# A written job list for the first seven blocks of an attention-and-two-MLPs kernel, two-place stores of split weights, and joined first loads

## The chip, the cores and the metric

The kernel runs on one core of a Trainium2 chip. A core has five engines that run their own queues of instructions in order and wait for each other by semaphores: TensorE (PE, with its weight loads PEld), VectorE (DVE), ScalarE (ACT), GpSimd (POOL) and SyncE (SP), which here issues DMAs. ACT can issue DMAs too. The metric is the device time of one execution in microseconds.

## The reference

Linear attention is followed by two MLPs. All arrays are float32.

```python
# q, k, v: (8 batches, 8 heads, 576, 64)
q_s = exp(q - max(q, -1)); q_s /= sum(q_s, -1) + 1e-9
k_s = exp(k - max(k, 2));  k_s /= sum(k_s, 2) + 1e-9
kv = einsum('bhsd,bhse->bhde', k_s, v)
attn = einsum('bhsd,bhde->bhse', q_s, kv)
x = attn.transpose(0, 2, 1, 3).reshape(4608, 512)
h = x @ w_in                          # (512, 2048)
x = (h * clip(h + 3, 0, 6) / 6) @ w_out      # first MLP
h = x @ w2_in
out = (h * sigmoid(h)) @ w2_out              # second MLP
```

## The kernel before

**Tiling.** The 4608 tokens are nine blocks (j) of 512. A unit u = 4j + pair is two heads of one block: its q, its share of k and v, and the kv product. One MLP step (phase, j, f) takes one of 16 slices of 128 hidden features: `mm1` makes h of the slice with 12 matmuls (four column groups c, three products each, since a float32 operand is held as an upper and a lower part), a gate makes g from h, and `mm2` adds the slice to the block's result with 12 matmuls.

**Stages.** `first_block` runs the attention of the first units, turns the first MLP's 32 weight tiles from float32 into parts, and runs steps (0, 0, f). `middle` runs blocks 1 to 6 and meanwhile prepares the second MLP's weights: sums of quarters of the matrices, split in parts and stored in the DRAM buffer `ws`. From block 4 on, x goes through DRAM too (`x_store`, `load_x`), then is split by ACT (`x_high`) and DVE (`x_low`). `second_mlp` does the rest in a seven-product form and is not touched.

**What sets the order.** `first_block` and `middle` write their work as jobs of a `Plan`: engine, time, key, function, jobs that must be done first. `Plan.run` plays the jobs through with these times, tries 400 random changes of the keys, and calls the functions in the best order that it found. Each engine then works off its instructions in that order.

**A unit's steps.** DVE takes the maxima (`q_max` L419, `k_max` L349 to L351); PE turns k's maxima (L356) and spreads them (L368); DVE and ACT make the exponentials (L377, L387); POOL subtracts and scales q (L427, L453); PE turns q (L461) and ACT copies it (L486); PE makes kv (L397), ACT scales it (L414), and PE makes x (`x_mm`, L495). ACT copies x's upper part (`x_upper`, L509). Its lower part comes in one of two ways: DVE subtracts (`x_lower`, L514, for the units in `DIRECT_X`), or PE adds minus the upper part into the same PSUM bank (`x_rest`, L522) and ACT copies what is left (`x_lower_copy`, L529). A gate has the same two ways: `lower` (L572, DVE, for the f in `DIRECT_G`) or `rest` (L584, PE) and `lower_copy` (L589, ACT). Before that, ACT applies relu (L554), DVE multiplies (`times_h`, L578) and ACT copies the upper part (L569).

**A weight tile's conversion.** ACT scales its two halves (L120, L124), DVE shifts, rounds and sets the sign (L132, L139, L143), ACT copies the upper part (L160), and DVE or, for the numbers in `ASIDE`, POOL subtracts for the lower part (L164).

**Loads.** k and v come in 512 rows and a tail of 64 rows, so a unit is one DMA for k, one for its tail, one for q, two for v and one for its tail: 256 + 64 + 256 + 256 + 64 = 896 KB. Units 2 and 3 go into the tile `ahead`. The weight tiles follow, 512 KB each.

**Spare matmuls.** `spin` puts matmuls without use (tile `busy`, L849) into the start.

## Time and profile before

| | us |
|---|---|
| median of 3 runs | 1578.11 (1577.84 to 1581.05) |
| profiled execution | 1579.01 |
| its span, first to last instruction | 1577.0 |
| PE busy | 1558.9 |
| DVE busy | 1111.1 |
| ACT busy | 761.6 |
| POOL busy | 487.8 |

The span is what the trace covers; the profiled execution is 2.0 us longer. Busy shares are averages over stages that differ much, so they have to be read by stage. A matmul's row lasts longer than the distance to the next one, since they overlap: it is the distance that counts in a row of matmuls. The same holds for DVE and ACT, where the next instruction can start before the last one's row has ended.

### The profile page before, as it was taken

The numbers are of one execution on the slowest core, as the hardware profiler recorded it, in microseconds if no ns is written. First come the engines' busy times: TensorE is split into PE (matmuls) and PEld (weight loads), VectorE is DVE, ScalarE is ACT, GpSimd is POOL, SyncE is SP. The second block draws the span as 40 slices with busy tenths as digits, with TensorE's granted clock in tenths as the row PEclk, the third lists the DMA queues.
The fourth block names the chain that finished last, engine by engine and source line by source line (L and its number), as shares of the span: only waits on it lengthen the run. The fifth ranks groups of instructions, "written<-read, shape, count | busy, mean of one in ns | idle before, by whom it ended". The sixth has DMA issues, their size and how long they took to land.

```text
span 1577.0 us, 22414 instructions
## 1 busy us (share of the span) xinstructions
PE 1558.9 (99%) x7352; PEld 1268.4 (80%) x7352; DVE 1111.1 (70%) x1792; ACT 761.6 (48%) x1360; POOL 487.8 (31%) x442
## 2 busy tenths in 40 slices
PE   7999999999999999999999999999999999999998
PEld 4777878887878888888888888888888888888887
DVE  7988577776767776554689569846986697677632
ACT  6886245454555554443365236533643464345322
POOL 4334224433424335321232243323223422440000
PEclk9999999999999999999999999999999999999999
DMA  9915977777778875755666786766668875879850
GB/s 267 345 44 185 313 216 227 238 215 215 223 215 246 235 227 166 238 174 193 192 222 218 214 226 224 249 217 192 237 203 218 220 252 192 227 226 370 260 127 27
DMA packets 391203, 342.82 MB, mean 217 GB/s; under 512 B 184880, under 2 KB 297520, under 8 KB 391088
## 3 DMA queue, kind: packets, MB, share of 16 engines
q1 hardware_dynamic: 389040, 340.32, 70.3%
q8 instruction: 58, 0.95, 0.2%
q10 hardware_dynamic: 2048, 1.08, 0.2%
q14 instruction: 57, 0.47, 0.1%
HBM read 247.20 MB, written 94.11 MB: 216 GB/s over the span
## 4 chain that ended last, share of the span: by engine, by line
PE 92%; DMA 2%; issue 1%; DVE 1%; POOL 1%; ACT 1%; SPq 1%; ACTq 0%; POOLq 0%; DVEq 0%
PE pb L1340 24%; PE pb L1499 24%; PE h L541 20%; PE y L613 17%; PE y L615 3%; PE pa L495 2%; PE pa L397 2%; DMA qraw<-in_q_dram 1%; DMA xr<-xq 0%; DMA xq<-xq 0%; POOL wi L164 0%; SPq L232 0%; PE pa L368 0%; PE pa L356 0%; ACT r L554 0%
## 5 line engine op out<-in xcount | busy, mean ns | idle before, releaser
L541 PE MATMUL h<-x,wi 128*128 128x512 f32 x1536 | 382.5, 396 | 1.6 <-POOL wi L164 0.9
L1340 PE MATMUL pb<-xo,ring 128*128 128x512 f32 x1680 | 383.0, 389 | 0.0
L1499 PE MATMUL pb<-gsp,ring 128*128 128x512 f32 x1680 | 382.4, 389 | 0.0
L1340 PEld LDWEIGHTS pb<-xo,ring 128*128 128x128 f32 x1680 | 315.4, 188 | 65.8 <-issue 0.5
L1499 PEld LDWEIGHTS pb<-gsp,ring 128*128 128x128 f32 x1680 | 315.4, 188 | 65.4
L541 PEld LDWEIGHTS h<-x,wi 128*128 128x128 f32 x1536 | 283.5, 188 | 65.9 <-POOL wi L164 2.0
L613 PE MATMUL y<-g,wo 128*128 128x512 f32 x1344 | 323.9, 390 | 0.6 <-ACT g L569 0.6
L613 PEld LDWEIGHTS y<-g,wo 128*128 128x128 f32 x1344 | 251.4, 188 | 53.6 <-ACT g L569 1.1
L1327 DVE TENSOR_TENSOR gsp<-g,gsp 128x512 fp32r<-128x512 f32 x240 | 183.0, 782 | 26.0 <-ACT gsp L1445 25.2
L1445 ACT CAST gsp<-g 128x512 fp32r<-128x512 f32 x240 | 143.6, 621 | 106.2 <-PE pb L1499 88.3
L578 DVE SCALAR_TENSOR_TENSOR h<-r,h 128x512 f32<-128x512 f32 x112 | 77.4, 691 | 80.3 <-ACT r L554 80.1
L554 ACT ACTIVATE r<-h 128x512 f32<-128x512 f32 x112 | 67.0, 598 | 133.4 <-PE h L541 131.7
L1327 POOL TENSOR_TENSOR xst<-xst 128x512 f32<-128x512 f32 x32 | 72.1, 2254 | 167.4 <-DVE xo L1327 85.3
L1327 DVE TENSOR_TENSOR g<-r,pb 128x512 f32<-128x512 f32 x96 | 65.7, 684 | 54.6 <-ACT r L1354 54.1
L1354 ACT ACTIVATE r<-pb 128x512 f32<-128x512 f32 x96 | 57.1, 595 | 97.0 <-DVE pb L1327 72.8
L1327 POOL TENSOR_TENSOR g<-g 128x512 f32<-128x512 f32 x40 | 53.6, 1340 | 148.6 <-DVE g L1327 123.4
L1327 POOL TENSOR_TENSOR s<-U,s 128x512 f32<-128x512 f32 x32 | 42.6, 1331 | 173.1 <-DVE U L1327 173.1
L569 ACT CAST g<-h 128x512 fp32r<-128x512 f32 x112 | 65.6, 586 | 59.8 <-DVE h L578 51.5
L572 DVE TENSOR_TENSOR g<-h,g 128x512 fp32r<-128x512 f32 x97 | 66.7, 688 | 28.8 <-ACT g L569 27.3
L1327 DVE TENSOR_TENSOR U<-pb,s 128x512 f32<-128x512 f32 x80 | 55.0, 688 | 17.0 <-PE pb L1340 14.9
L194 POOL TENSOR_TENSOR fa<-fa 128x256 f32<-128x256 f32 x64 | 49.9, 780 | 43.7 <-DVE sp L226 28.5
L427 POOL TENSOR_TENSOR qe<-qraw,qm 128x512 f32<-128x512 f32 x34 | 37.9, 1114 | 79.4 <-DVE qz L469 46.0
(158 smaller groups left out, 1721.2 us busy)
## 6 DMA issues: line engine op xcount, KB each, us to landing
ring<-ws SPq DMA_DIRECT2D x280, 512.0 KB, 3.9
ws<-sp SPq DMA_DIRECT2D x256, 128.0 KB, 2.6
wi_early<-in_moe_w_in_dram SPq DMA_DIRECT2D x16, 512.0 KB, 8.6
wo_early<-in_moe_w_out_dram SPq DMA_DIRECT2D x16, 512.0 KB, 9.6
wi_raw<-in_moe_w_in_dram SPq DMA_DIRECT2D x16, 512.0 KB, 5.0
ws<-w_sum SPq DMA_DIRECT2D x64, 128.0 KB, 2.2
ws<-fa SPq DMA_DIRECT2D x64, 128.0 KB, 2.3
wo_raw<-in_moe_w_out_dram SPq DMA_DIRECT2D x16, 512.0 KB, 4.4
```

The lines of the kernel that those rows point to most:

```text
L194: lambda to=to, x=x, y=y, op=op: nc.gpsimd.tensor_tensor(out=at[to], in0=at[x], in1=at[y], op=op)
L541: nc.tensor.matmul(h, w[:, a, c, :], x[:, e, c, :], start=(c == 0 and n == 0), stop=(c == NC - 1 and n == 2),)
L554: nc.scalar.activation(self.r, self.h, AF.Relu, bias=3.0)
L569: nc.scalar.copy(self.g[:, 0], self.r)
L572: nc.vector.tensor_tensor(out=self.g[:, 1], in0=self.r, in1=f32(self.g[:, 0]), op=ALU.subtract)
L578: nc.vector.scalar_tensor_tensor(out=self.h, in0=self.r, scalar=6.0, in1=self.h, op0=ALU.min, op1=ALU.mult)
L613: nc.tensor.matmul(y[c], w[:, a, cs], g[:, e, :], start=st, stop=sp)
L1327: (eng or nc.vector).tensor_tensor(out=out, in0=a, in1=b, op=how)
L1340: nc.tensor.matmul(to, ws_[:, a], e[:, c], start=p in ("P1", "P6", "P5") and c == 0 and m == 0, stop=c == 1 and m == 2, skip_group_check=True,
L1354: nc.scalar.activation(r, d[b, n, key], AF.Sigmoid)
L1445: nc.scalar.copy(t[0], source(p, i))
L1499: nc.tensor.matmul(d[b, p][m], w[:, a, m * P : (m + 1) * P], t[e], start=new and i == 0 and k == 0, stop=i == NPR - 1 and k == 2, skip_gro ...
```

## The change

The order is no longer searched. `FIRST` and `MIDDLE` are written lists of job numbers, two signs for each job, and `run` calls the jobs in that order. The order has been found outside of the kernel. With it go four other edits. More of the lower parts are subtracted by DVE: `DIRECT_X` has six units instead of two, `DIRECT_G` eleven f instead of one, and `ASIDE` gives POOL 18 weight tiles instead of 16. `store` of a split weight writes the two places in `ws` of one part in one DMA of 256 KB instead of two of 128 KB. The first loads are joined: k and q of units 2 and 3 in one DMA each, the tails of two units in one, and ACT issues q of units 0 and 1, v of unit 0 and a tail. There are six kv tiles instead of five, one more tile for `k_max`, other waits between kv jobs, and 27 spare matmuls instead of 31.

```diff
+FIRST = (
+    "000503020A0108060B040F070J0b090M0c0C0G0N0H1b0a0O0D0d0e0P0I0f1F0K0E0Q0v0h0L1c0S0i1t0R0z0g0T0U1i1G0j0m"
...
+MIDDLE = (
+    "L809AWCGAe0XL9AYAXCELAAf020GLBAg0VK-AZLCLDAwAaLE00K_AxAbLFAy01LcL0L20AEE03Ac0BLI0W04AzLJ0C05LKAh0DLL"
...
-    KVS = NP + 1
+    KVS = NP + 2
...
+    halved = const.tile([P, 2 * P], F32, name="halved")
...
         def store(self):
-            for h, name in enumerate(self.names):
-                to = ws[self.ph, self.o, slot(self.o, self.i, name)]
-                for a, t in enumerate((self.hi, self.lo)):
-                    nc.sync.dma_start(
-                        to[:, a * HALF : (a + 1) * HALF], f32(t)[:, h * HALF : (h + 1) * HALF]
-                    )
+            s0, s1 = (slot(self.o, self.i, name) for name in self.names)
+            to = ws[self.ph, self.o, min(s0, s1) : max(s0, s1) + 1 : abs(s1 - s0)]
+            to = to.rearrange("s p d -> p s d")
+            for a, t in enumerate((self.hi, self.lo)):
+                halves = f32(t).rearrange("p (h d) -> p h d", h=2)
+                nc.sync.dma_start(
+                    to[:, :, a * HALF : (a + 1) * HALF], halves if s0 < s1 else halves[:, ::-1]
+                )
...
+            order = [DIGITS.index(table[n]) * 64 + DIGITS.index(table[n + 1]) for n in range(0, len(table), 2)]
+            done = set()
+            for i in order:
+                assert i not in done and done.issuperset(jobs[i][4])
+                done.add(i)
+                fn = jobs[i][3]
+                (fn[0] if jobs[i][0] in ("SP", "AQ") else fn)()
+                if after:
+                    after(i)
...
-    DIRECT_X = (1, 2)
-    DIRECT_G = (14,)
-    ASIDE = (0, 2, 3, 4, 7, 9, 10, 11, 14, 17, 20, 22, 23, 24, 26, 27)
+    DIRECT_X = (0, 1, 4, 5, 6, 7)
+    DIRECT_G = (2, 3, 6, 8, 9, 10, 11, 12, 13, 14, 15)
+    ASIDE = (0, 2, 3, 4, 6, 7, 10, 11, 12, 13, 14, 16, 18, 19, 20, 21, 23, 25)
+
+    FROM_ACT = ("kt0", "v0", "q1")
+
+    SPIN_FIRST = 10
     SPIN = {
...
+        38: 2, 17: 4, 20: 5, 28: 1, 62: 2, 70: 2, 72: 1,
     }
...
+        k0 = begin_load("k0", 0.5, s0, main_k, K, 0, 1)
+        kt0 = begin_load("kt0", 0.6, s0 + 0.1, tails, 2 * T, k, 0)
...
+        k2 = begin_load("k2", 0.6, s0 + 2.0, main_k, 2 * K, 2, 2)
+        kt2 = begin_load("kt2", 0.6, s0 + 2.1, tails, 2 * T, k, 2)
+        n_q[2] = n_q[3] = begin_load("q2", 0.6, s0 + 2.2, main_q, 2 * Q, 2, 2)
+        v2 = begin_load("v2", 1.2, s0 + 2.3, main_v, V, 2)
...
-                    [kx, n_v.get(u), xmm.get(u - 1)], ["a"], ["ke"],
+                    [kx, n_v.get(u)], ["a"], ["ke"],
...
-        for fn in plan.run(0, 300e3):
-            fn()
+        plan.run(MIDDLE)
```

The order is shown at three places. The first is SP at the start of the program: the loads of units 2 and 3 (`ahead`) and the first weight tile (`wi_early`). Before, these rows follow six others with the loads of units 0 and 1:

```order
L311 DMA vbuf<-in_v_dram 64x2x64
L296 DMA ahead<-in_k_dram 128x2x256
L300 DMA ahead<-in_k_dram 64x2x64
L322 DMA ahead<-in_q_dram 128x2x256
L307 DMA ahead<-in_v_dram 128x4x64 x2
L311 DMA ahead<-in_v_dram 64x2x64
L296 DMA ahead<-in_k_dram 128x2x256
L300 DMA ahead<-in_k_dram 64x2x64
L322 DMA ahead<-in_q_dram 128x2x256
L307 DMA ahead<-in_v_dram 128x4x64 x2
L311 DMA ahead<-in_v_dram 64x2x64
L105 DMA wi_early<-in_moe_w_in_dram 128x4x256
```

Now these are SP's first rows:

```order
L861 DMA kbuf<-in_k_dram 128x2x256 x2
L875 DMA ahead<-in_k_dram 64x4x64
L868 DMA vbuf<-in_v_dram 128x4x64 x2
L884 DMA ahead<-in_q_dram 128x4x256
L875 DMA vbuf<-in_v_dram 64x4x64
L861 DMA ahead<-in_k_dram 128x4x256
L868 DMA ahead<-in_v_dram 128x4x64 x2
L177 DMA wi_early<-in_moe_w_in_dram 128x4x256
L875 DMA ahead<-in_v_dram 64x4x64
L868 DMA ahead<-in_v_dram 128x4x64 x2
L171 DMA wo_early<-in_moe_w_out_dram 128x1024
```

The first weight tile's load has moved from behind 20 DMAs on SP and 4 on ACT to behind 10 on SP and 5 on ACT, ahead of unit 3's v.

The second place is ACT from the first weight tile on. Before, the conversion of the first tile starts there, and the last part of unit 3's x is a `CAST x` behind the rows shown:

```order
L120 ACTIVATE fa<-wi_early 128x512
L124 ACTIVATE fr<-wi_early 128x512
L387 ACTIVATE ke<-ke 128x640
L486 COPY qt<-pa 128x512
L120 ACTIVATE fa<-wo_early 128x512
L124 ACTIVATE fr<-wo_early 128x512
L414 ACTIVATE kv_95<-pk,small 64x64 x2
L509 CAST x<-pa 128x512
L486 COPY qt<-pa 128x512
L387 ACTIVATE ke<-ke 128x640
L437 ACTIVATE qe<-qe 128x512
L509 CAST x<-pa 128x512
```

Now, from the same conversion on:

```order
L192 ACTIVATE fa<-wi_early 128x512
L196 ACTIVATE fr<-wi_early 128x512
L580 CAST x<-pa 128x512
L557 COPY qt<-pa 128x512
L485 ACTIVATE kv_95<-pk,small 64x64 x2
L508 ACTIVATE qe<-qe 128x512
L192 ACTIVATE fa<-wo_early 128x512
L196 ACTIVATE fr<-wo_early 128x512
L459 ACTIVATE ke<-ke 128x640
L557 COPY qt<-pa 128x512
L580 CAST x<-pa 128x512
L459 ACTIVATE ke<-ke 128x640
```

The conversion has moved ahead of unit 0's and unit 1's x; from it to the last part of unit 3's x there were 27 instructions on ACT, and now there are 30.

The third place is DVE in the first block, in the row of conversions (`ISA` is the round, L139 before and L211 now; the numbers behind names tell tiles apart). Before, about ten gates in:

```order
L132 TENSOR_SCALAR fa_1045<-fa_1045 128x512
L139 ISA fa_1045<-fa_1045,fr_1047 128x1024
L143 SCALAR_TENSOR_TENSOR fa_1045<-wi_early_129,fa_1045 128x512
L132 TENSOR_SCALAR fa_1101<-fa_1101 128x512
L139 ISA fa_1101<-fa_1101,fr_1103 128x1024
L143 SCALAR_TENSOR_TENSOR fa_1101<-wi_early_131,fa_1101 128x512
L442 TENSOR_REDUCE qs_1162<-qe_1110 128x8
L578 SCALAR_TENSOR_TENSOR h_1112<-r_1159,h_1112 128x512
```

Now, some gates in:

```order
L215 SCALAR_TENSOR_TENSOR fa_672<-wi_early_116,fa_672 128x512
L204 TENSOR_SCALAR fa_713<-fa_713 128x512
L649 SCALAR_TENSOR_TENSOR h_680<-r_732,h_680 128x512
L211 ISA fa_713<-fa_713,fr_715 128x1024
L236 TENSOR_TENSOR wi_750<-fa_672,wi_750 128x512
L215 SCALAR_TENSOR_TENSOR fa_713<-wi_early_118,fa_713 128x512
L643 TENSOR_TENSOR g_765<-h_680,g_765 128x512
L204 TENSOR_SCALAR fa_738<-fa_738 128x512
L204 TENSOR_SCALAR fa_773<-fa_773 128x512
L211 ISA fa_738<-fa_738,fr_740 128x1024
L211 ISA fa_773<-fa_773,fr_775 128x1024
```

Shift, round and sign of one tile no longer stand next to each other: among the first 33 tiles, a round directly behind its own shift falls from 23 to 3, and a sign directly behind its own round from 27 to 0. The gate's lower part (`g<-h,g`) stands among them.

Counted over the whole program, PE has 14 fewer `minus` matmuls (L584: 15 to 5, L522: 6 to 2), ACT has 14 fewer copies, DVE has 14 more subtracts for g and x and 2 fewer for weights, POOL has 2 more, and SP has 199 fewer DMAs, 192 of them stores to `ws`.

## Rows read from the trace of the kernel before

**Rows 1.** Page, part 1: busy time, share of the span and instructions of each engine.

```profile
PE 1558.9 (99%) x7352; PEld 1268.4 (80%) x7352; DVE 1111.1 (70%) x1792; ACT 761.6 (48%) x1360; POOL 487.8 (31%) x442
```

**Rows 2.** Busy time of each engine in five stretches (us from the start).

```profile
core 0: us, PE busy (x) PEld busy (x) DVE busy (x) ACT busy (x) POOL busy (x), PEclk, DMA share, GB/s
0.00:35.00 35.00, 26.05 (x156) 15.60 (x157) 27.03 (x68) 22.44 (x42) 13.05 (x24) 1.00 0.91 264
35.00:60.00 25.00, 24.43 (x105) 18.99 (x104) 24.15 (x40) 21.91 (x41) 9.32 (x8) 1.00 1.04 381
60.00:150.00 90.00, 89.56 (x477) 70.30 (x478) 80.20 (x146) 72.68 (x136) 31.73 (x30) 1.00 0.43 137
150.00:725.00 575.00, 571.33 (x2878) 461.85 (x2878) 387.75 (x674) 275.28 (x496) 212.03 (x237) 1.00 0.74 221
725.00:1560.00 835.00, 835.00 (x3686) 691.63 (x3685) 587.48 (x859) 365.33 (x640) 221.65 (x144) 1.00 0.71 220
```

**Rows 3.** Timeline of PE: start, duration, instruction, idle before it and its releaser.

```profile
34.77 3.64 PE L541 MATMUL h<-x,wi 128*128 128x512 f32 x14 [0.44 <-ACT x L529]
38.25 0.39 PE L584 MATMUL h<-g,minus 128*128 128x512 f32 x1
38.47 2.88 PE L613 MATMUL y<-g,wo 128*128 128x512 f32 x12
```

**Rows 4.** Chain of waits in the first 62 us: start, length, what.

```profile
0.79 3.61 DMA qraw<-in_q_dram
...
12.51 3.62 DMA ahead<-in_q_dram
```

**Rows 5.** Timeline of SP's queue: the issue of the first weight tile's load.

```profile
15.16 0.59 SPq L105 DMA_DIRECT2D wi_early<-in_moe_w_in_dram  x1
```

**Rows 6.** Timeline of ACT: first conversion, and the last parts of unit 3's x.

```profile
19.72 0.67 ACT L120 ACTIVATE fa<-wi_early 128x512 f32<-128x512 f32 x1 [2.39 <-DMA wi_early<-in_moe_w_in_dram]
20.29 0.67 ACT L124 ACTIVATE fr<-wi_early 128x512 uint32<-128x512 uint32 x1
...
32.96 0.59 ACT L509 CAST x<-pa 128x512 fp32r<-128x512 f32 x1
33.44 0.62 ACT L160 CAST wi<-fa 128x512 fp32r<-128x512 f32 x1
34.13 0.59 ACT L529 CAST x<-pa 128x512 fp32r<-128x512 f32 x1
34.67 0.62 ACT L160 CAST wo<-fa 128x512 fp32r<-128x512 f32 x1
```

**Rows 7.** Timeline of DVE: conversions that follow each other, and others.

```profile
34.55 1.51 DVE L132 TENSOR_SCALAR fa<-fa 128x512 uint32<-128x512 uint32 x1
...
82.07 0.42 DVE L132 TENSOR_SCALAR fa<-fa 128x512 uint32<-128x512 uint32 x1
82.52 0.69 DVE L139 CUSTOM_DVE_ANT_0 fa<-fa,fr 128x1024 uint16<-128x1024 uint16 x1
83.25 0.69 DVE L143 SCALAR_TENSOR_TENSOR fa<-wo_early,fa 128x512 uint32<-128x512 uint32 x1
...
84.41 0.69 DVE L139 CUSTOM_DVE_ANT_0 fa<-fa,fr 128x1024 uint16<-128x1024 uint16 x1
85.02 0.68 DVE L442 TENSOR_REDUCE qs<-qe 128x8 f32<-128x512 f32 x1
...
87.14 0.38 DVE L132 TENSOR_SCALAR fa<-fa 128x512 uint32<-128x512 uint32 x1
87.43 0.68 DVE L419 TENSOR_REDUCE qm<-qraw 128x8 f32<-128x512 f32 x1
```

**Rows 8.** Chain of waits in the middle: start, length, what.

```profile
350.19 5.28 DMA xq<-xq
359.54 5.48 DMA xr<-xq
```

**Rows 9.** Timeline of PE: the longest idle time after the first block.

```profile
464.19 0.30 PE L356 MATMUL pa<-ident,peaks 128*128 128x128 f32 x1 [2.07 <-DVE peaks L351]
```

294 lines of the change are left out of this document (160 added, 134 removed).

## The prediction

> **What bounds the kernel now.** I read the page's first part first: PE is busy for 99% of the span [rows 1], so only two things can save time, work taken off PE and the stretches in which PE waits. The busy times by stage say where the latter lie [rows 2]. PE is idle for 35.00 - 26.05 = 8.95 us before 35 us, 0.57 us from 35 to 60, 0.44 us from 60 to 150, 3.67 us from 150 to 725, and not at all from there to 1560. The change reaches the first four stretches. The first has more in it than its idle time: 31 spare matmuls lie there too, so what counts is when the stream of matmuls becomes dense.
>
> The timeline of PE tells that [rows 3]. Step 0's `mm1` needs the x of all four units; its last three matmuls and all of step 1's run as one piece from 34.77 us, after a wait for ACT's L529, the last part of unit 3's x. From there PE has 0.57 + 0.44 us of waits in 115 us. So the first quantity is the time at which unit 3's x is ready, 34.7 us now, and the second the work in the dense stream.
>
> Why 34.7? The chain of waits begins with loads. The q load of unit 3 is issued at 12.51 us and lands 3.62 us later; the very first one took 3.61 us on empty queues [rows 4]. So the early loads wait for their turn on SP more than for bandwidth. The first weight tile is issued at 15.16 us [rows 5], and ACT, which had waited 2.39 us for it, begins with it at 19.72 us [rows 6]. From there to 34.67 us, where the L529 that matters has made way for the next row, ACT works off 27 instructions in 14.95 us, 0.55 us each with what it waits.
>
> **Start: the loads.** Ahead of the first weight tile stood 4 units of 896 KB, with itself 4096 KB; now, by the order, 3008 KB of loads stand ahead, with itself 3520 KB (3.60 MB), behind 10 issues on SP instead of 20. Bounds for its landing: the rate at which the old loads arrived (4.19 MB from 0.79 to 19.72 us, 221 GB/s) gives 0.79 + 16.3 = 17.1 us; the mean rate of the first 35 us, 264 GB/s [rows 2], gives 0.79 + 13.6 = 14.4 us. I take the middle, 15.7, because the old loads did not fill the queues but the new ones still come in short pieces.
>
> A rule of the Trainium skill speaks against any gain in rate: "DMA: Bandwidth & Descriptors", section Specifications, wants at least 512 bytes in a piece for full rate, and the pieces of v and of the tails stay at 256 bytes, joined or not. By that rule the landing is the slow bound, 17.1 us, and the total 1.4 us more, 1572.6 us. No row here separates the rate of long pieces from that of short ones.
>
> **Start: ACT.** From the same conversion to the last part of unit 3's x there are now 30 instructions, three more, since unit 0's and 1's x stand behind it. At 0.55 us with waits they take 16.6 us; at the distances of unhindered rows (0.57 us from L120 to L124, 0.48 from L509 to L160, 0.54 from L529 to L160 [rows 6]) the mix takes some 14.8 us. I take 16.0 us: 15.7 + 16.0 = 31.7 us against 34.7, **3.0 us less**. Both bounds together give 29.2 to 33.7 us, a gain of 1.0 to 5.5 us. The k, q and v of unit 3 come from other queues: POOL's scale of its q and DVE's maximum stand earlier in their rows than before, and I cost them at nothing as long as ACT is the one that is full.
>
> **Dense stream: matmuls removed.** Ten of 15 L584 and four of six L522 go; the two L522 that stay run ahead of the dense part, as two did before. From L584 to the next matmul is 38.47 - 38.25 = 0.22 us [rows 3], so 14 x 0.22 = **3.1 us less** on PE, which waits for almost nothing there. The spare matmuls fill waits and count for nothing at either number.
>
> **Dense stream: what takes their place.** Each removed matmul and its copy on ACT becomes one subtract on DVE; two weight subtracts go from DVE to POOL. So DVE has 12 more rows of about 0.61 us (the distance from the round at 84.41 to the next row [rows 7]), 7.3 us. DVE is the second fullest engine: free for 0.85 us of 35 to 60 and 9.8 us of 60 to 150 [rows 2]. But the order also pulls shift, round and sign of a tile apart. Next to each other, shift to round takes 0.45 us and round to sign 0.73; with other work between, shift to next is 0.29 and round to next 0.61 [rows 7]. With 20 and 27 such neighbours fewer that is 20 x 0.16 + 27 x 0.12 = 6.4 us. Net, DVE has 0.9 us more, and 3.1 us less time for it as PE's stream shortens: 4.0 us out of 10.6 free. I cost it at nothing; were that cover gone, each subtract would cost PE its 0.61 us. ACT is relieved by 14 copies. POOL was busy for 31.73 of 90 us [rows 2], so two more subtracts are hidden.
>
> **Middle.** SP issues 192 stores fewer, but SP ends no wait of PE there: the chain shows round trips through DRAM, x's store and its reload, 5.28 and 5.48 us [rows 8], and the longest idle time, 2.07 us, was a wait for DVE's maximum [rows 9], which stood behind such a reload in DVE's row. The trace cannot tell how the new list places these waits. Bounds: all 3.67 us gone, or as much again added. I take 0.8 us less, as half the stores leave SP more room ahead of a reload.
>
> **Small edits.** One more kv tile to clear, one more tile for `k_max`, the freed waits of kv: nothing, they lie beside the first loads or lengthen no row. The joined tail makes unit 0 wait for a 64 KB load that also brings unit 1's tail; the extra 32 KB is 0.15 us at 221 GB/s, inside the bounds above.
>
> **Sum.** 1579.0 of the profiled execution - 3.0 - 3.1 - 0.8 = 1572.1 us. The profiled execution is 0.9 us above the median of the runs, so the median to expect is **1571.2 us**. About 0.2% (3.2 us, 1574.9 to 1581.3) is what a measurement can tell from no change.
>
> **Rivals.**
>
> *The start gains nothing* (0.12). The loads land no earlier in effect, or another engine in unit 3's chain takes ACT's place. For it: the new order has unit 0's subtraction of k behind the q maxima of units 2 and 3 on DVE, so the first unit's chain waits for a later load. Against it: unit 0 is not the last one. It gives 1571.2 + 3.0 = 1574.2 us.
>
> *DVE becomes the bound of the first block* (0.13). For it: DVE has almost no free time from 35 to 60 us, and POOL's subtracts hold it up: the shift at 34.55 took 1.51 instead of 0.42 us [rows 7], beside a POOL subtract. With 10.6 us free and 7.3 + 3.1 = 10.4 needed, the new DVE work fits only just if pulling the tiles apart saves nothing, and an engine that works in order loses some of its free time; half of 10.4 us lost makes 1571.2 + 5.2 = 1576.4 us. The Trainium skill ("SBUF — State Buffer", section SBUF: two separate sides) has the pair of ports that DVE and POOL share as a lock held for a whole instruction. By it, two more POOL subtracts can each stop DVE once more; the row above shows 1.1 us for one such stop.
>
> *A reload comes late in the middle* (0.09). Blocks 4 to 6 get x back through DRAM. If in the new list the reload's issue stands behind an SP instruction that waits for a late release, the block's `mm1` waits for one trip, 5.4 us [rows 8]. Two blocks hit cost 10.8 us, against 6.1 us gained in the first block: 1578.1 + 4.7, about 1582 us. It decides from two on; one hit leaves 1577.4 us. Against it: the stores are half as many, so less stands ahead.
>
> *The middle's idle time goes altogether* (0.11). The list places each reload and maximum early enough: 2.9 us more, 1568.3 us.
>
> **How the numbers follow.** The forecast has 0.55, with a range of its own from 1568 to 1574.5 by the bounds of start and middle. Faster by over 0.2%: 0.55 + 0.11, a good half of the first rival (0.07) and a little of the second (0.03), 0.76. Within 0.2%: the rest of these two and of the third, 0.05 + 0.10 + 0.01 = 0.16. Slower: 0.08. The range for 8 in 10 leaves out the third rival and the best of the fourth: 1567 to 1577 us.
>
> **What would show it.** Right: the first conversion begins on ACT near 15.7 us, and the long piece of `mm1` near 31.8; PE's idle time from there to 150 us stays about 1 us; L584 and L522 count 14 fewer. DVE's rounds are followed by other work within 0.61 us. Wrong: PE waits for DVE's g (the subtract for `DIRECT_G`) or for a weight's lower part between 60 and 130 us, which is the second rival; a conversion that begins before 16 us while the long piece still begins at 34 us, which is the first; PE idle for more than 5 us between 150 and 725 us behind x reloads, which is the third.

## The result, and the profile after

| | before | after |
|---|---|---|
| median of the runs, us | 1579.24 (4 runs) | 1596.83 (1592.54 to 1599.23, 4 runs) |
| profiled execution, us | 1579.01 | 1594.71 |
| its span, us | 1577.0 | 1593.0 |

The ratio is 1.0108 [1.0079, 1.0136]: the changed kernel is **slower** by 17.6 us. The prediction said 1571.2 us, faster. The experiments were measured in rounds, each with the kernel before beside them; its median lay between 1577.9 and 1579.8 us from round to round, and the four runs of the changed kernel lie 6.7 us apart. A difference of two medians below some 3 us is therefore not read here unless the traces show its place. Ratios are to the kernel before of the same round.

The page's first part for the changed kernel (engine, busy time, share of the span, instructions) answers to [rows 1]:

```profile
PE 1558.7 (98%) x7334; PEld 1266.9 (80%) x7334; DVE 1117.6 (70%) x1803; ACT 755.3 (47%) x1346; POOL 499.2 (31%) x444
```

PE has 18 instructions fewer, 14 of them the `minus` matmuls, and yet is busy as long as before. The busy times by stage, in the columns of [rows 2], with the part from 150 to 550 us apart:

```profile
0.00:35.00 35.00, 25.43 (x150) 16.64 (x150) 25.26 (x65) 21.37 (x41) 15.76 (x25) 0.90 0.92 267
35.00:60.00 25.00, 20.84 (x112) 15.85 (x113) 23.53 (x42) 18.70 (x36) 10.26 (x9) 0.86 1.08 358
60.00:150.00 90.00, 87.59 (x439) 69.89 (x439) 86.32 (x153) 68.19 (x124) 33.97 (x26) 1.00 0.38 119
150.00:550.00 400.00, 386.43 (x1985) 309.27 (x1984) 294.05 (x523) 193.81 (x354) 189.21 (x214) 1.00 0.81 246
```

Four figures differ from [rows 2]. PE's idle time is 4.16 instead of 0.57 us from 35 to 60, 2.41 instead of 0.44 from 60 to 150, and 13.57 us from 150 to 550, where all the 3.67 us of [rows 2] lay before. And the granted clock, 1.00 throughout before, is 0.90 and 0.86 in the first two stretches. From 725 us on PE is busy for all of the time, as before.

Because the two kernels order their work differently, windows of time compare different work. A second measure helps: the time at which the n-th matmul of `mm1` and `mm2` begins, counted from the start of the span. The table gives its distance to the kernel before (positive is later; n = 384 ends the first block, 2304 lies behind the middle), for the kernels that the text needs most:

| n | 12 | 60 | 384 | 1536 | 2304 | last |
|---|---|---|---|---|---|---|
| before, us | 35.34 | 47.41 | 138.74 | 433.43 | 633.07 | 1566.69 |
| after | +2.7 | +10.1 | +4.5 | +19.2 | +16.2 | +16.2 |
| e1 | +3.0 | +10.9 | +5.3 | +3.8 | +0.5 | +19.0 |
| e2 | +8.1 | +9.6 | +13.1 | +31.6 | +28.7 | +28.7 |
| e4 | +0.8 | +0.7 | +0.7 | -0.2 | -3.4 | -3.4 |
| e5 | +7.1 | +7.0 | +6.6 | +21.4 | +20.5 | +20.5 |
| e6 | +1.8 | +7.4 | +1.8 | +20.9 | +17.6 | +17.6 |
| e7 | -0.6 | +6.4 | +4.1 | +19.5 | +17.4 | +17.5 |
| e9 | -2.2 | +5.0 | -0.6 | +16.8 | +13.0 | +13.0 |
| e13 | -1.8 | +3.8 | -1.7 | -5.0 | -9.7 | -9.7 |
| e18 | +0.2 | +0.1 | -0.3 | -3.1 | -7.9 | -7.9 |

The row of the changed kernel says: the first block ends 4.5 us late instead of 6.1 early, and the middle loses 14.7 us more by n = 1536, at 433 us of the kernel before. Two faults, then, which the experiments take one at a time. Each row is one trace. The same first block ended at +4.5, +5.3, +4.9 and +6.8 us in four of them (the changed kernel, e1, e8 and e10), so a microsecond or two in this table can be chance.

What the start looks like in the changed kernel: rows of SP's queue, ACT and PE (start, duration, engine, line, operation, and in brackets the idle time before it and its releaser).

```profile
9.30 1.18 SPq L177 DMA_DIRECT2D wi_early<-in_moe_w_in_dram  x1
13.94 0.62 SPq L875 DMA_DIRECT2D ahead<-in_v_dram  x1
16.26 1.22 SPq L868 DMA_DIRECT2D ahead<-in_v_dram  x2
17.53 0.61 SPq L171 DMA_DIRECT2D wo_early<-in_moe_w_out_dram  x1
```

```profile
16.62 0.69 ACT L192 ACTIVATE fa<-wi_early 128x512 f32<-128x512 f32 x1
21.82 0.67 ACT L192 ACTIVATE fa<-wo_early 128x512 f32<-128x512 f32 x1 [1.68 <-DMA wo_early<-in_moe_w_out_dram]
34.10 0.58 ACT L600 CAST x<-pa 128x512 fp32r<-128x512 f32 x1
```

```profile
36.58 4.91 PE L612 MATMUL h<-x,wi 128*128 128x512 f32 x15
52.06 0.29 PE L440 MATMUL pa<-ident,small 128*128 128x128 f32 x1 [3.09 <-DVE small L434]
52.82 4.86 PE L684 MATMUL y<-g,wo 128*128 128x512 f32 x12
```

The first weight tile is issued at 9.30 us, 5.9 earlier than in [rows 5], and its conversion begins 3.1 us earlier than in [rows 6]. Still the last part of unit 3's x (L600) comes at 34.10 us, and the long piece of `mm1` at 36.58 instead of 34.77 [rows 3]. Behind the issue of `wi_early` SP does nothing for 3.5 us, then nothing for 1.7 us more. And the first dense pieces are slow: 15 matmuls in 4.91 us, 12 in 4.86, where [rows 3] has 14 in 3.64 and 12 in 2.88. Part of each ran at the lower of the two levels, 1.2 GHz, behind a wait of PE (1.98 us at 35.68, 3.09 us at 52.06). In a stretch of the second piece the granted clock was 0.50:

```profile
52.90:56.20 3.30, 3.30 (x9) 2.31 (x8) 3.30 (x7) 3.30 (x7) 0.00 (x0) 0.50 1.09 407
```

In the middle PE waits for gates above all. The two largest of its waits from 150 to 725 us (total, times, longest) make 9.5 of 13.8 us; the other 4.3 are waits for DVE, 4.0 of them ahead of turning and spreading the maxima of k:

```profile
PE y L684 <- ACT g L640: 6.1, 4, 3.4
PE h L612 <- DVE g L643: 3.4, 4, 1.6
```

### The profile page after: what moved, and what is told of

It is laid out like the page before. It is cut to its first block, busy times and chain, and to the rows that moved or that the text cites. A ratio compares the mean times of both kernels' runs of the same rounds, so it can differ in the third digit from the quotient of the medians.

```text
span 1593.0 us, 22107 instructions
## 1 busy us (share of the span) xinstructions
PE 1558.7 (98%) x7334; PEld 1266.9 (80%) x7334; DVE 1117.6 (70%) x1803; ACT 755.3 (47%) x1346; POOL 499.2 (31%) x444
## 4 chain that ended last, share of the span: by engine, by line
PE 87%; DVE 5%; DMA 3%; issue 1%; ACT 1%; POOL 1%; SPq 1%; ACTq 0%; DVEq 0%; POOLq 0%
PE pb L1395 24%; PE pb L1554 24%; PE h L612 18%; PE y L684 16%; PE y L686 3%; PE pa L566 2%; PE pa L468 1%; DMA qraw<-in_q_dram 1%; DMA xr<-xq 1%; DVE fa L215 1%; DMA kbuf<-in_k_dram 0%; DVE h L649 0%; DVE ke L449 0%; DVE peaks L422 0%; DVE qm L490 0%
## 5 line engine op out<-in xcount | busy, mean ns | idle before, releaser
L684 PE MATMUL y<-g,wo 128*128 128x512 f32 x1344 | 333.7, 397 | 6.5 <-ACT g L640 6.1
L625 ACT ACTIVATE r<-h 128x512 f32<-128x512 f32 x112 | 66.8, 597 | 118.3 <-PE h L612 113.9
L643 DVE TENSOR_TENSOR g<-h,g 128x512 fp32r<-128x512 f32 x107 | 73.2, 685 | 32.2 <-ACT g L640 30.6
L1382 DVE TENSOR_TENSOR U<-pb,s 128x512 f32<-128x512 f32 x80 | 55.0, 688 | 19.1 <-PE pb L1395 12.8
L1409 ACT ACTIVATE r<-s 128x512 f32<-128x512 f32 x32 | 20.2, 633 | 87.3 <-POOL s L1382 70.3
```

What stands on the lines that cost most here:

```text
L625: nc.scalar.activation(self.r, self.h, AF.Relu, bias=3.0)
L643: nc.vector.tensor_tensor(out=self.g[:, 1], in0=self.r, in1=f32(self.g[:, 0]), op=ALU.subtract)
L684: nc.tensor.matmul(y[c], w[:, a, cs], g[:, e, :], start=st, stop=sp)
L1382: (eng or nc.vector).tensor_tensor(out=out, in0=a, in1=b, op=how)
L1409: nc.scalar.activation(r, d[b, n, key], AF.Sigmoid)
```

## Experiments: which part costs the time

**e1, e2, e3: each list, or both, replaced.** The jobs stay as changed; the order is had by playing them through with their keys, as before.

```diff
-        plan.run(FIRST, lambda i: spin(SPIN.get(i, 0)))
+        plan.run(None, lambda i: spin(SPIN.get(i, 0)))
...
-        plan.run(MIDDLE)
+        plan.run(None)
```

> The changed kernel, but the order of its middle is found as in the kernel before (the jobs are played through once with their planned times), not read from the list MIDDLE; jobs, stores and the first block stay. Theory 'middle list': of the 16.0 us that the changed kernel lost, 10.3 us are PE's idle time between 150 and 725 us (13.95 us against 3.67), and the written order causes them; then this run gives about 10 us back, 1586 to 1588 us, with 3 to 5 us idle in that stretch. Rival 'middle's jobs': the two-place stores or the other waits between kv jobs cause them; then the order doesn't matter and it stays within 3 us of 1596.8 us.

> The changed kernel, but the order of its first block is found by playing the jobs through, not read from FIRST; the joined loads, the sets of subtracts on DVE and POOL, the spare matmuls (tied to the same jobs) and the list MIDDLE stay. Theory 'first list': the 5 to 6 us that were lost ahead of 150 us come from the written order; then about 1591 us. Rival 'loads and subtracts': they come from the joined loads and from more work on DVE; then 1596 us or more, and the long piece of mm1 begins no earlier than 36 us.

> The changed kernel with both orders found by playing the jobs through, so that of the change only the two-place stores, the joined loads, the sets DIRECT_X, DIRECT_G and ASIDE, the sixth kv tile and the spare matmuls are left. If both lists cause the loss and the rest gains the 3.1 us of removed matmuls: 1576 to 1582 us. If the lists add to what the rest costs: 1582 to 1590 us. If the lists are innocent: 1596 us.

Measured (e2 has the first edit above, e1 the second, e3 both): e1 1596.56 us, ratio 1.0112 [1.0095, 1.0129]; e2 1606.16, 1.0175 [1.0160, 1.0190]; e3 1609.96, 1.0199 [1.0184, 1.0215]. e2 came out with its rival, 1596 us or more, and e3 lies 14 us above the highest of its forecasts. The total of e1 is that of the changed kernel, as its rival had it, but not for the rival's reason: its time is lost elsewhere. Two windows of e1, columns as above, and its largest wait behind them (total, times, longest):

```profile
150.00:550.00 400.00, 397.65 (x2087) 321.50 (x2087) 288.82 (x525) 196.06 (x359) 171.84 (x198) 1.00 0.78 237
550.00:725.00 175.00, 161.14 (x750) 128.86 (x749) 94.97 (x148) 75.47 (x132) 44.10 (x45) 0.94 0.59 181
```

```profile
PE y L685 <- ACT o L702: 11.8, 2, 7.3
```

With the order played, idle time from 150 to 550 us falls from 13.57 to 2.35 us, so the list `MIDDLE` does carry the loss of that stretch; the played order instead has a stall of its own at a block's end, behind n = 2304. For the changed jobs, then, `MIDDLE` is worth nothing against the order played, while `FIRST` is worth 1606.2 - 1596.8 = 9.3 us.

**e4: before, with the two-place stores alone.**

```diff
-            for h, name in enumerate(self.names):
...
+            to = ws[self.ph, self.o, min(s0, s1) : max(s0, s1) + 1 : abs(s1 - s0)]
```

> The kernel before with one part of the change: split weights are stored two places at a time, 192 stores fewer. If a store of 256 KB holds up nothing, as predicted: within 1.5 us of the kernel before, 1577.5 to 1580.5 us. If the larger stores delay the loads and reloads behind them on the queues: slower by 3 to 10 us, with waits for reloads in the middle.

Measured: 1574.63 us (10 runs), 0.9974 [0.9965, 0.9983]: 4.2 us gained, where no change or a loss was expected. The reload that [rows 9] hung on shows how: before, SP issued it at 457.31 us and DVE's row behind it waited 3.04 us; in e4 it is issued at 451.88 and that wait is gone. First the kernel before, SP and DVE, then e4, SP:

```profile
457.31 0.45 SPq L671 DMA_DIRECT2D xr<-xq  x1
462.36 0.69 DVE L663 TENSOR_TENSOR x<-xr,x 128x512 fp32r<-128x512 f32 x1 [3.04 <-ACT x L659]
```

```profile
451.88 0.50 SPq L673 DMA_DIRECT2D xr<-xq  x1
```

e4's idle time from 150 to 550 us is 0.44 us, against 3.67.

**e5: the changed kernel with the first block of before** (its jobs, loads, sets of units and spare matmuls; stores and `MIDDLE` as changed).

```diff
-    DIRECT_G = (2, 3, 6, 8, 9, 10, 11, 12, 13, 14, 15)
+    DIRECT_G = (14,)
...
-        plan.run(FIRST, lambda i: spin(SPIN.get(i, 0)))
+        plan.run(None)
```

> The changed kernel with the first block of the kernel before: its loads, its sets DIRECT_X, DIRECT_G and ASIDE, its spare matmuls and its order, played through; two-place stores, six kv tiles and the list MIDDLE stay. Counting the mm1 and mm2 matmuls of the first block and the middle, the changed kernel reaches matmul 384 (the end of the first block) 4.5 us later than the kernel before, and matmul 2304 (block 6) 16.2 us later. If the first block and the list MIDDLE cost time independently: 1596.8 - 4.5 = about 1592 us, and against the kernel before with two-place stores (1574.6 us) the list MIDDLE costs some 15 to 17 us. If the list only suffers from a first block that leaves it in another state: under 1583 us.

Measured: 1599.27 us, 1.0120 [1.0103, 1.0138], more than either forecast. The old first block doesn't cure it: the middle loses as much behind it (13.9 us from n = 384 to the end, by the table, against 11.7). But this first block itself ended 6.6 us late, though its order was the old one; it shares with the changed kernel the new layout of k and v in the tile `ahead`. Its loads are not joined, and yet SP waits there for the landing of earlier loads, which led to e9 (SP's waits up to 25 us: total, times, longest):

```profile
SPq L386 <- DMA ahead<-in_v_dram: 5.5, 2, 3.0
```

## Experiments: the first block

**e9: tails of v in a place of their own.** In the changed kernel the tail of v of units 2 and 3 lies in `ahead` between the main parts. SP's issue of the tail waits until unit 2's main part has landed, and the next main part's issue until the tail has: that is the gap from 9.30 to 17.53 us above. e9 puts both tails behind all main parts.

```diff
-    vfar = ahead[:, KB : KB + VB].rearrange("p (u h j d) -> p u h j d", h=2, j=KCH + 1, d=D + 1)
+    VM = AHEAD * 2 * KCH * (D + 1)
+    vfar = ahead[:, KB : KB + VM].rearrange("p (u h j d) -> p u h j d", h=2, j=KCH, d=D + 1)
+    vend = ahead[:, KB + VM : KB + VB].rearrange("p (u h d) -> p u h d", h=2, d=D + 1)
```

> The changed kernel with the tails of v of units 2 and 3 in a place of their own in the tile ahead, behind the main parts; same DMAs in the same order. In the changed kernel the tails lie between the main parts, and SP's issue of that tail waits for the landing of unit 2's main part (3.4 us at 10.6 us), the next issue for the landing of the tail (1.6 us). Theory 'false wait': without them SP issues the load of wo 0 about 4 us earlier than 17.5 us, ACT's wait of 1.7 us for it goes, and mm1's long piece (36.58 us) begins 1 to 3 us earlier: 1594 to 1596 us. Rival: only the order of the bytes on the queues counts, the weight lands no earlier and the piece begins at 36.5 us: 1597 us.

Measured: 1592.30 us, 1.0083 [1.0067, 1.0100]; 4.5 us less than the changed kernel, though the two intervals of the ratio still overlap. SP, ACT and PE of e9, against the rows above:

```profile
9.50 1.17 SPq L177 DMA_DIRECT2D wi_early<-in_moe_w_in_dram  x1
10.72 1.19 SPq L879 DMA_DIRECT2D ahead<-in_v_dram  x1
11.96 1.29 SPq L872 DMA_DIRECT2D ahead<-in_v_dram  x2
13.29 0.62 SPq L171 DMA_DIRECT2D wo_early<-in_moe_w_out_dram  x1
```

```profile
20.34 0.67 ACT L192 ACTIVATE fa<-wo_early 128x512 f32<-128x512 f32 x1
31.84 0.58 ACT L601 CAST x<-pa 128x512 fp32r<-128x512 f32 x1
```

```profile
32.33 3.67 PE L613 MATMUL h<-x,wi 128*128 128x512 f32 x15
46.96 0.29 PE L440 MATMUL pa<-ident,small 128*128 128x128 f32 x1 [3.50 <-DVE small L434]
```

`wo_early` is issued 4.2 us earlier, ACT no longer waits for it, unit 3's x comes at 31.84 us (the prediction had 31.7) and the long piece at 32.33 with 15 matmuls in 3.67 us. Shown, then: about 5 us of the first block were lost through a wait of one load for another that it doesn't depend on. The traces bear it out over their scatter: with the tails between, the first block ended 4.5 to 6.8 us late in four traces, with the tails apart at -0.6, -1.7 and +2.5 us in three (e9, e13, e17).

**e11: does an earlier weight tile help before?** e4 with the first two weight loads ahead of other loads on SP.

```diff
-"SP", 0.55, -10.0 + 0.9 * f
+"SP", 0.55, -27.45 + 0.01 * o if f == 0 else -10.0 + 0.9 * f
```

> The kernel before with two-place stores (1574.6 us) and one more edit: the loads of the first two weight tiles are issued ahead of unit 3's loads instead of behind them. If ACT, from the first conversion on, is what unit 3's x waits for, as the prediction had it, the first conversion begins about 3 us earlier (some 17 us instead of 20.4) and the long piece of mm1 2 to 3 us earlier: 1572 us. If unit 3's loads, now 1.3 us later, set the end instead: 1574 to 1576 us.

Measured: 1586.59 us, 1.0046 [1.0031, 1.0061]; slower than e4 by 12 us. The issue went from 16.02 us in e4 to 11.47, the landing from 20.4 to 16.0; the first conversion moved only from 20.39 to 20.08 us. ACT, which in e4 had waited 1.74 us for the tile, no longer waits there, but begins hardly earlier: other work stands ahead of the conversion in ACT's order. An earlier landing alone is worth nothing at that start; the changed key also changed the played order, and why that lost 12 us stays open.

**e12: the larger sets alone** (e4 with the changed `DIRECT_X`, `DIRECT_G`, `ASIDE`, order played).

```diff
-    DIRECT_G = (14,)
+    DIRECT_G = (2, 3, 6, 8, 9, 10, 11, 12, 13, 14, 15)
```

> The kernel before with two-place stores (1574.6 us) and the sets DIRECT_X, DIRECT_G and ASIDE of the change: 14 matmuls and 14 ACT copies less, 12 DVE subtracts and 2 POOL subtracts more in the first block; loads, spare matmuls' counts and the played order's rule stay (the three spare matmuls behind x_rest of unit 0 go with it). Theory 'DVE has room', as predicted: 1574.6 - 3.1 = 1571.5 us. Rival 'DVE is the bound of the first block': PE waits for g and for weights' lower parts between 35 and 150 us, 4 to 10 us in all, 1576 to 1582 us.

Measured: 1585.46 us, 1.0037 [1.0024, 1.0050]; 10.8 us slower than e4. PE's window and its largest waits from 60 to 150 us:

```profile
60.00:150.00 90.00, 81.88 (x414) 63.38 (x413) 82.95 (x149) 64.93 (x120) 26.34 (x23) 0.98 0.31 93
```

```profile
PE pa L358 <- DVE peaks L353: 2.1, 1, 2.1
PE h L543 <- ACT g L591: 1.9, 2, 1.2
```

14 matmuls fewer, and 8.12 us of waits in this stretch: 3.6 us of those listed are for DVE (the maxima and g), 3.8 for ACT. The larger sets do not pay in the played order. How much of that is the subtracts on DVE, and how much an order that fits them badly, is not shown. With `FIRST` PE waits 2.4 us there.

**e6: spare matmuls in the waits of PE** (32 more, no use made of their results).

```diff
-        38: 2, 17: 4, 20: 5, 28: 1, 62: 2, 70: 2, 72: 1,
+        38: 2, 17: 4, 20: 5, 28: 1, 62: 2, 70: 10, 72: 1, 99: 9, 341: 15,
```

> The changed kernel with 32 spare matmuls more, put into three waits of PE: 8 after q_turn of unit 2 (idle at 21.6 to 23.7 us), 9 before unit 4's k_turn (33.7 to 35.7 us) and 15 before unit 5's k_spread (49.0 to 52.1 us; these add zero to a bank). No other instruction moves. Theory 'clock': the three stretches of half clock (mm1 x6 in 2.14 us, mm1 x15 in 4.91, mm2 x12 in 4.86) follow from PE standing idle before them; then the granted clock is 1.00 from 35 to 60 us, the 12 matmuls of mm2 at 53 us take 2.9 us, and 3 to 4 us are given back: 1593 us. Rival: the clock falls for another reason, or the spare matmuls run into the work behind the waits: 1596 to 1599 us.

Measured: 1594.64 us, 1.0091 [1.0076, 1.0106], not to be told from the changed kernel in total. The window, and the second piece:

```profile
35.00:60.00 25.00, 24.44 (x142) 18.91 (x141) 24.80 (x46) 20.01 (x38) 10.40 (x8) 1.00 1.07 353
```

```profile
51.70 3.26 PE L685 MATMUL y<-g,wo 128*128 128x512 f32 x12
```

The clock is 1.00 instead of 0.86, the pieces take 3.70 and 3.26 us instead of 4.91 and 4.86, and the first block ends 2.7 us earlier. In the total that is gone again: the middle of this trace loses 15.8 us behind n = 384, against 11.7.

**e7: the spread of unit 4's maxima later in PE's order.** The wait of 3.09 us at 52.06 is for it; e7 puts the jobs that lead to unit 4's and 5's kv behind `mm2` of step 0 and the gate of step 1.

```diff
-FIRST: 330 331 333 334 340 343 375 344 345 346 357 358
+FIRST: 449 343 375 ... 453 330 331 333 334 454 340 456 344 345 459 346 357 467 358
```

> The changed kernel with a few jobs of FIRST moved: unit 4's k_turn, k_peak, k_spread, k_sub, k_exp behind mm1 of step 1, its kv product behind mm2 of step 0, its x_mm and unit 5's k_spread behind mm2 of step 1. Theory 'PE's order': ready matmuls stood behind a matmul that waits for DVE, 1.98 + 0.38 us at 33.7 us and 3.09 us at 49.0 us, each with half clock behind it (1.3 and 2.0 us); then mm1's long piece begins by 35.2 us, both waits shrink under 1 us, and 6 to 8 us are given back: 1589 to 1591 us. Rival 'DVE is the bound': the matmuls in front wait for the same full DVE one step later, and it stays above 1594 us.

Measured: 1597.52 us, 1.0109 [1.0085, 1.0134]. The start gained 3.3 us (n = 12), of which 0.4 was left at n = 384. In the window from 60 to 150 us DVE has 86.32 of 90 us taken in the changed kernel and 87.00 in e7, so the work moved meets a DVE that is full; that this is where the gain went is argued, not shown. DVE's and POOL's rows ahead of the wait of 3.09 us in the changed kernel show DVE held up as well:

```profile
47.65 1.79 DVE L215 SCALAR_TENSOR_TENSOR fa<-wo_early,fa 128x512 uint32<-128x512 uint32 x1
50.55 1.17 DVE L204 TENSOR_SCALAR fa<-fa 128x512 uint32<-128x512 uint32 x1
```

```profile
47.26 1.63 POOL L236 TENSOR_TENSOR wo<-fa,wo 128x512 fp32r<-128x512 f32 x1 [2.86 <-ACT wo L232]
```

A sign of 1.79 us instead of 0.69 [rows 7] and a shift of 1.17 instead of 0.42, beside POOL's subtracts at 47.26 and 50.16 us: about 1.9 us of DVE's time in the 5 us ahead of the reduction for which PE waits (`small`, 51.63 us).

## Experiments: the middle

**e8: without POOL's sums.** In the middle POOL is busy for 189 us of 400, and DVE's rows beside it are stretched.

```diff
-                done = [add("POOL", 0.68, at + 1.3, fn, done, [], [], True)]
+                done = [add("POOL", 0.68, at + 1.3, lambda: None, done, [], [], True)]
...
-                done = [add("POOL", 0.68, at + 2.3 + 0.1 * m, fn, done, [], [], True)]
+                done = [add("POOL", 0.68, at + 2.3 + 0.1 * m, lambda: None, done, [], [], True)]
```

> The changed kernel without the sums of quarters on POOL in the middle (64 subtracts or adds of 0.77 us, so the second MLP computes with wrong weights); nothing else is left out. Theory 'POOL holds DVE up': in the changed kernel POOL works 65 + 62 us in 150 to 350 us instead of 32 + 41, and DVE's rows beside it take 0.5 to 1.1 us longer; PE's 13.6 us of idle time in 150 to 550 us then fall to 5 us or less, 1586 to 1589 us. Rival 'queues': the waits come from reloads and copies that stand ahead of a gate in ACT's and SP's rows, and the idle time stays above 10 us, 1593 us or more.

Measured: 1595.73 us, 1.0095 [1.0077, 1.0113]. The window:

```profile
150.00:550.00 400.00, 387.64 (x1986) 310.50 (x1985) 285.15 (x524) 192.19 (x354) 108.00 (x110) 0.99 0.81 246
```

POOL 81 us less, DVE 9 us less, PE's idle time 12.36 instead of 13.57 us. POOL's sums aren't the cause.

**e10: one stall followed to its place.** In the changed kernel PE waits 3.41 us at 441.71 for ACT's copy of g, and ACT had stood still for 5.47 us:

```profile
441.71 4.61 PE L684 MATMUL y<-g,wo 128*128 128x512 f32 x12 [3.41 <-ACT g L640]
```

```profile
438.34 0.62 ACT L730 CAST x<-xr 128x512 fp32r<-128x512 f32 x1 [5.47 <-PE h L612]
438.86 0.59 ACT L625 ACTIVATE r<-h 128x512 f32<-128x512 f32 x1
```

L730 is `x_high`, the upper part of block 5's x; it overwrites a tile that `mm1` of block 3 reads. The list runs `mm1` of block 3's step 15 ahead of steps 13 and 14, and puts `x_high` behind step 15's but ahead of those of 13 and 14. They too read the tile, so ACT stands until their 24 matmuls have ended, with the relu of step 13 (L625) queued behind. e10 puts `x_high` behind the relu of step 14, and another pair of the same kind behind its gate. (Here and for e7 the edit is shown in job numbers; the list has two signs for each.)

```diff
-MIDDLE: 318 ... 319 ... 345 ... 1832 ... 262 ... 1744 ... 1745 ... 263
+MIDDLE: 1832 318 319 345 ... 1744 262 ... 1745 263
```

> The changed kernel with five jobs of MIDDLE moved: x_high and x_low of unit 20 and the reload behind them go behind the relu of step (0, 3, 14); x_high and x_low of unit 18 go behind the upper part and the lower part of step (0, 3, 4)'s gate. Theory 'one job ahead of a gate': the list runs mm1 of step 15 of block 3 ahead of steps 13 and 14, so the x tile is not free when x_high of the next block stands in ACT's row; it holds up the relu behind it, PE's 3.41 us at 438 us with half clock behind it (12 matmuls in 4.61 us), and the same with a reload at 369 us (1.51 us). Then PE has no wait over 1 us at these two places and 6 to 7 us are given back: 1590 to 1591 us. Rival: the gate is late for DVE's or SP's sake as well and waits 2 to 3 us anyway: 1594 us or more.

Measured: 1596.12 us, 1.0106 [1.0084, 1.0127], no difference in total. PE's rows at the place:

```profile
441.61 2.88 PE L678 MATMUL y<-g,wo 128*128 128x512 f32 x12
448.78 1.65 PE L606 MATMUL h<-x,wi 128*128 128x512 f32 x6 [1.52 <-DVE g L637]
```

The wait is gone and 12 matmuls take 2.88 instead of 4.61 us. The 4.61 had the lower level of the clock in it, as this window of the changed kernel shows:

```profile
442.00:445.30 3.30, 3.30 (x9) 2.51 (x9) 3.10 (x7) 1.18 (x3) 0.00 (x0) 0.50 0.77 218
```

But a wait of 1.52 us for DVE's g is new. From n = 1440 to 1536 the changed kernel falls 6.4 us further behind (12.8 to 19.2), e10 2.9 (16.0 to 18.9): 3.5 us gained here. In the same run the first block ended 2.3 us later than in the changed kernel's (n = 384: +6.8), and behind n = 1536 it won back 1.5 us less. One place of several; 6 to 7 us had been expected of both places.

**e17: gates first.** e9 with some 60 jobs of ACT and DVE that stood ahead of a late relu or product of a gate put behind it.

```diff
-MIDDLE: ... job, relu or times_h ...
+MIDDLE: ... relu or times_h, job ...
```

> The changed kernel with the tails of v apart (1592.3 us) and MIDDLE rearranged: where the trace of the changed kernel shows a gate's relu or multiply starting over 0.8 us after its input was ready, the jobs that stood ahead of it in its engine's row after that moment go behind it, with what depends on them; 60 moves in all, everything else keeps its order. Theory 'gates behind other work': the played order keeps an engine free for a gate that is about to be ready, the written one does not; then PE's idle time from 150 to 550 us (14.4 us with the tails apart) falls to 7 us or less and the time to 1582 to 1586 us. Rival: the gates are late because of buffers and loads, or the work moved behind is missed as badly elsewhere: over 10 us idle, 1589 us or more.

Measured: 1594.01 us, 1.0096 [1.0079, 1.0113], against e9's 1592.30:

```profile
150.00:550.00 400.00, 383.19 (x1970) 306.33 (x1969) 289.83 (x519) 191.07 (x350) 187.35 (x212) 1.00 0.79 244
```

Idle time grew to 16.81 us. PE's waits are still for gates above all. So the simple mend fails: moving what stands ahead of a late gate does not give the time back. Whether the gates are late for another reason or the moved work is missed elsewhere, this run can't tell.

## Experiments: both faults taken out

**e13: e9 with the middle of before** (the conditions between its jobs, its keys, order played; the first block with `FIRST`, stores as changed). The conditions act on how an order is played, not on the instructions that a job makes. So behind the first block e9 and e13 have the same instructions in another order.

```diff
-                    "DVE", 1.1, key(0), lambda: k_max(u), [n_k.get(u)], ["m1"]
+                    "DVE", 1.1, key(0), lambda: k_max(u), [n_k.get(u)], ["m1", "t2k"], ["t2k"], True
...
-        plan.run(MIDDLE)
+        plan.run(None)
```

> The changed kernel with the tails of v apart, its first block by the list FIRST, but with the middle of the kernel before: its jobs and its order, played through; two-place stores stay. If the order of MIDDLE is what costs the time after 150 us, whatever the first block hands over: the mended first block ended 1.25 us ahead of the one of the kernel before with two-place stores (1574.6 us), so 1573.3 us, 19 us under the same first block with the list. If the new first block hands over something that disturbs the middle: 1580 us or more.

Measured: 1569.71 us (1568.55 to 1570.53, 5 runs), 0.9949 [0.9936, 0.9961]: **faster than both kernels**. Page part 1 of e9 and then of e13, and three stretches of e13:

```profile
PE 1557.1 (98%) x7334; PEld 1264.3 (80%) x7334; DVE 1115.6 (70%) x1804; ACT 754.6 (47%) x1346; POOL 499.6 (31%) x444
PE 1548.1 (99%) x7334; PEld 1263.4 (81%) x7334; DVE 1118.6 (71%) x1804; ACT 753.8 (48%) x1346; POOL 499.7 (32%) x444
```

```profile
35.00:60.00 25.00, 21.50 (x130) 16.89 (x129) 24.77 (x44) 21.48 (x42) 10.13 (x7) 1.00 1.07 358
60.00:150.00 90.00, 87.53 (x441) 69.88 (x440) 87.15 (x151) 65.94 (x120) 38.48 (x31) 1.00 0.45 144
150.00:550.00 400.00, 399.56 (x2098) 324.38 (x2097) 286.89 (x518) 198.04 (x364) 153.77 (x177) 1.00 0.79 238
```

Against e9, which has the same first block, the list `MIDDLE` costs 1592.3 - 1569.7 = **22.6 us** (20.6 if each is taken against the kernel before of its own round, 22.7 in the traces). How it costs them can be read from the two pages, with the same 7334 instructions on PE: spans of 1589.7 and 1567.0 us, PE busy for 1557.1 and 1548.1. Of the 22.7 us between them 13.7 are idle time, 9.0 are the same instructions taking longer, as in the 4.61 instead of 2.88 us of e10's place.

e1 tells more beside e13. Both play the order of the middle; they differ in the place of v's tails and in the conditions between the middle's jobs (what has to be free for `k_max`, and the waits between kv jobs). Behind n = 384 e1 loses 13.8 us and e13 wins 8.0. So the changed conditions lead the played order to a loss of the same size as the list's.

**e14 and e16: two cross-checks.** e14 is e13 with 15 spare matmuls at the 3.50 us wait; e16 is e9 with them and with e10's moves.

```diff
-        38: 2, 17: 4, 20: 5, 28: 1, 62: 2, 70: 2, 72: 1,
+        38: 2, 17: 4, 20: 5, 28: 1, 62: 2, 70: 2, 72: 1, 341: 15,
```

> As the run before it, with 15 spare matmuls (they add zero to a bank) ahead of unit 5's k_spread, where PE waits 3.5 us at 43 us for DVE and the granted clock falls to 0.93 of full in 35 to 60 us. If half clock behind this wait costs what the trace shows (mm2 x12 in 4.7 instead of 2.9 us): 1.8 us less, 1571.5 us. If the spare matmuls run into ready work: 1573.3 us or more.

> The changed kernel with three mends and both lists: tails of v apart (1592.3 us), 15 spare matmuls ahead of unit 5's k_spread, and x_high behind the gate at the two places in the middle. If each gives what its stretch shows (1.8 and 3.5 us): 1587 us. If the middle's other waits take it back: 1590 us or more.

Measured: e14 1570.20 us, 0.9952 [0.9940, 0.9965], the same as e13, whose clock was 1.00 behind that wait without them; there was nothing to give back. e16 1587.63 us, 1.0072 [1.0057, 1.0088], 4.7 us less than e9 in the medians, but 2.7 if each is taken against the kernel before of its own round, and the intervals overlap. That the mends add up is likely, not shown; most of the middle's loss remains.

**e18: e4 with kv's last product over all rows.** e13 gains more than its first block and stores explain: by the table it wins 7.98 us behind n = 384, e4 4.10. One edit had been passed over: the fifth part of a unit's keys, 64 rows, is now multiplied over 128 rows, the empty ones holding zeros.

```diff
-            n = P if j < KCH else TAIL
...
-                    t[0:n, j, d], tv[0:n, j, h, :]
+                    t[:, j, d], tv[:, j, h, :]
```

> The kernel before with two-place stores (1574.6 us) and one more edit, taken from the change: the kv product's tail is multiplied over all 128 rows, with the rows behind the tail's 64 set to zero, instead of over 64 rows. Theory 'row counts': each of the 32 kv products takes 0.145 us less on PE, which waits for almost nothing after 35 us: 32 x 0.145 = 4.6 us, 1570.0 us. Rival: the shorter products only make PE wait for something else: 1573 to 1575 us.

Measured: 1570.80 us, 0.9951 [0.9937, 0.9964], 3.8 us less than e4 (2.9 against the kernel before of its own round, 4.4 in the traces). A kv product and what follows it, before and then e13:

```profile
153.14 0.95 PE L397 MATMUL pa<-vbuf,ke 128*64 128x65 f32 x20 [0.44 <-ACT ke L387]
154.02 8.50 PE L613 MATMUL y<-g,wo 128*128 128x512 f32 x36
```

```profile
150.99 0.80 PE L469 MATMUL pa<-vbuf,ke 128*64 128x65 f32 x20 [0.44 <-ACT ke L460]
151.72 8.45 PE L686 MATMUL y<-g,wo 128*128 128x512 f32 x36
```

From the first of its 20 matmuls to the next other one a product holds PE for 0.88 us before and 0.73 with full rows, in e18 as in e13. The mean difference over the program is 0.145 us; 32 such products would give 4.6 us, and 3 to 4 came.

## Why the prediction was wrong, point by point

The changed kernel is e13 plus two faults: 1569.7 + 22.6 (middle) + 4.5 (the false wait at the start) = 1596.8 us. The sum closes by construction, since both terms are differences of these runs. That e13 lies near the predicted 1571.2 us proves little, since it gets there by other terms.

**The middle, -0.8 with bounds of 3.67 us either way: this step failed.** The list measured +22.6 us against the middle's order of before with the same stores. The bound was taken from the idle time of the kernel before, and a new order isn't bounded by what the old one idles: it can put any instruction in front of any other. The order was at hand, row by row, and its places were not searched for what e10 shows, a job that overwrites a tile ahead of jobs that still read it. The third rival, a loss in the middle, was the nearest, but by another mechanism (a reload late on SP, about 10.8 us) and for half the price. Half of its sign came, more than 5 us of idle time, but PE waits for gates and for DVE's maxima, not for reloads. Shown is that the order costs the time; e10 shows one place, about 3.5 us; e8 excludes POOL's sums, e17 the simple mend. How the rest of the 22.6 us divides over the places **stays open**.

On POOL the Trainium skill ("SBUF — State Buffer", section SBUF: two separate sides) has the port pair that DVE and POOL share held for a whole instruction. The stretched rows at 47.65 and 50.55 agree; in the middle, leaving out POOL's 64 sums took only 1.2 us off PE's idle time (e8).

**The loads, -3.0: the landing right, what ACT waits for wrong.** The first weight tile landed at 15.1 us (issued at 9.30, 5.8 us on its way), against 15.7 predicted; the slow bound of 17.1 us didn't come. That is closer than the working deserves: a tail is 32 KB for each unit (64 rows of two heads), not 64, so a unit is 832 KB and not 896; with 3.93 MB instead of 4.19 the same working gives 18.1 us for the slow bound and 16.3 for the middle. The conversion began at 16.62 us, for ACT was busy until then. From there to the last part of unit 3's x ACT took 17.5 us instead of 16.0. What failed is the sentence that costs unit 3's k, q and v "at nothing as long as ACT is the one that is full": SP's loads behind the tile waited for each other's landing. With that out (e9) the same stretch took 14.9 us, and unit 3's x stood at 31.84 us against 31.7, the long piece at 32.33 against 31.8. That this fits so well is luck: ACT began 1.2 us late and was 1.1 us quicker. Nor does e11 bear out that the landing of that tile sets the start.

**The matmuls, -3.1, and the cover on DVE: half right.** 14 matmuls fewer are there. The cover wasn't: of 90 us from 60 to 150 DVE is busy for 86.32 instead of the 81 or so expected from [rows 2], and PE idles 2.41 instead of 0.44 us. In the played order the same sets cost 10.8 us (e12). The first two terms together were to make the first block 6.1 us shorter; mended, it ends 0.6 and 1.7 us earlier in e9 and e13, 2.5 later in e17. In e13 PE idles for 5.97 us from 35 to 150 us, against 1.01 before, and every wait listed there is for DVE. The largest:

```profile
PE pa L441 <- DVE small L435: 3.5, 1, 3.5
```

The second rival, DVE as the bound, is thus part of the truth, at about its price: 5.0 us more idle time, 5.2 was named. Its sign was another one: only 0.7 us of these waits are for DVE's g, the rest for the maxima of k and for x.

**"The spare matmuls fill waits and count for nothing": failed.** 27 instead of 31 left waits in which PE did nothing; behind them matmuls ran at 1.2 GHz for a time, and 32 more gave 2.7 us back in the first block of one trace (e6). In e13 the same wait had no such stretch behind it.

**The stores: right in kind, wrong in size.** Half as many issues left SP room ahead of a reload, as said; worth 4.2 us (e4), not 0.8: 3.2 of the 3.67 us of idle time from 150 us on went, not a fifth. The fourth rival, whose sign this is, came true for the stores alone.

**"Small edits: nothing": failed.** The kv product over full rows is worth 3 to 4 us (e18); it stands in the kernel's code, and neither the description of the change nor the prediction names it. The changed conditions between the middle's jobs, put at nothing, make the played order 21.7 us slower (e1 beside e13).

Two sentences ahead of the prediction are wrong. A unit's loads are 832 KB, as above. And the search tries no random changes of the keys: 400 is what `run` does unless told otherwise, but both calls ask for none (`plan.run(0, 300e3)`), so the order before is one play-through.
